# Two constants of a kernel's planner: a later count for GpSimd's copies, and a shorter lead for scores

## The chip, the core and the metric

The kernel runs on one core of one Trainium2 chip. The metric is the device time of one execution in microseconds (us); lower is better. A core has five engines that each work through their own list of instructions in order and meet at semaphores: TensorE (PE in the profile; its weight loads are shown apart as PEld), VectorE (DVE), ScalarE (ACT), GpSimd (POOL) and SyncE (SP, which here only issues DMAs).

## The reference

Attention with talking heads, and a feed-forward layer behind it:

```python
scores = scale * np.matmul(q, k.transpose(0, 1, 3, 2))        # 8 batches, 12 heads, 448 x 448, head_dim 64
scores = np.einsum('bhij,hg->bgij', scores, w_pre)            # heads are mixed before the softmax
attn = softmax(scores, axis=-1)
attn = np.einsum('bhij,hg->bgij', attn, w_post)               # and after it
x = np.matmul(attn, v)                                        # -> 3584 tokens x 768
h = np.maximum(x @ w_in, 0.0)                                 # 768 -> 2048
out = h * h @ w_out                                           # 2048 -> 768
```

## The kernel before

**The work.** Each of the 8 batches is cut into 45 chunks of ten query rows for all twelve heads (120 rows of the array; a few chunks are smaller). A chunk goes through a fixed sequence:

- scores by matmul (L732) into PSUM, copied to SBUF as `snat` by VectorE or ScalarE (L533, L535); there are two `snat` buffers, and a new block of scores may be copied in only when the relayouts that read the old one have landed;
- a relayout by DMA from `snat` into one of 14 buffers `sch` (L763, issued by SP), so that the twelve heads of ten queries lie in one tile;
- the mix of heads by matmul (L892, or in pairs on quarter arrays L838), the row minimum on VectorE (`mn`, L903), the exponential on ScalarE (`es`, L906), the reciprocal of the sums on VectorE (`rc`, L913, once for two chunks);
- scaling of the mixing weights by that reciprocal on GpSimd (`wq`, L916, one instruction for a chunk);
- the matmul of `wq` and `es` (L923, four for a chunk; the text calls it the second mix), its eviction (`atb`), and with all chunks of a half the product with the values (L969).

The feed-forward layer (L1028 for w_in, L1067 for w_out, squares on GpSimd L1049) works on 128 to 256 tokens at a time; it is TensorE's filler between the chunks. The mode in which TensorE's array is split changes with the operation: L838 and most of L732 run on quarter arrays (four matmuls side by side), L969 on two halves, all others on the whole array.

**Keys and queries.** From batch 2 on (`x_piece`), keys and queries of a batch come in two pieces of six heads. GpSimd copies each piece into pair order, three copies for keys (`kn`) and three for queries (`qn`), L659. Then SP issues a transposing DMA of the piece (L672 into `kt`, L678 into `qz`). There is one `kn` and one `qn`, so that the copies of a piece must wait until the transpose of the piece before has landed; each `kt` and `qz` has two buffers, one for each piece, so that a transpose must wait until the scores of the batch before have read them.

**Order.** The kernel has no loop whose order is the program's order. All operations are added to a planner with a list of what they depend on, a cost in ns for each engine and a priority. `Planner.run` plays them against a clock of its own: an engine takes the ready operation of the lowest priority number, is busy for its cost, and what depends on it becomes ready after a further latency. The order in which the planner started the operations is the order that each engine gets. Its costs and latencies are thus used only to choose that order; on the chip each instruction waits for its real semaphores. Three points matter:

- `AHEAD` (7.7) is the number of chunks by which scores (L737) and relayouts (L777, L797) run ahead of the mix that they serve, in the priority.
- A copy of keys or queries depends on the load (`k_in`, `q_in`) and on the transpose of the piece before (`tk_op`, `tq_op`). `ck` and `cq` are the lists of these copies. `NEAR_LAST` (2e6) is their priority; scaling has about its chunk's number, the feed-forward squares 1e6, so of all that is ready on GpSimd the copies come last.
- While TensorE would idle in the first 130 us of the planner's clock, and its share of work is low, the planner puts in matmuls on zeroes (`still`, L1292), which only keep the array at work.

Of the kernel before, what the change touches and what calls it, by code (L numbers as in the profile page):

```python
# [39 lines left out]
NEAR, TURN_SP = {"POOL": 640}, 1500  # L40
PIECE = NPAIR // 2
NE = 6
NSCH = 14
AHEAD = 7.7
FIFO = 50
IDLE_NS, IDLE_COLS, IDLE_FROM, IDLE_END, IDLE_LOW = 112, 256, 1300, 130000, 0.62
SPELL, PHASE, DROP, RISE = 3413, 1700, 0.4, 0.8
# [5 lines left out]
LATER = 2  # L53
ONSET, ONSET_IDLE, ONSET_FROM = 2500, 2500, 20000
NEAR_LAST = 2e6
OSTEP = 2
GS, ONE = [(0, 1, 2)], [(0,), (1,), (2,)]
STAY = {ROWS: 2, COLS: 6, BOTH: 8}
# [69 lines left out]
class Planner:  # L128
# [8 lines left out]
    def add(self, eng, ns, pri, fn, deps=(), lat=60, bank=None, frees=None, mode=0):  # L137
        op = Op(eng if isinstance(eng, dict) else {eng: ns}, lat, pri, fn, list(deps), bank, frees, mode)
        self.ops.append(op)
        return op  # L140
# [199 lines left out]
def kernel(  # L340
# [199 lines left out]
    add = pl.add  # L540
# [13 lines left out]
    q_in, k_in, v_in = {}, {}, {}  # L554
    def keep(key, fn):
        def go(*got):
            for key_, slot in zip(key if isinstance(key, list) else [key], got):
                slots[key_] = slot
            fn(*got)
        return go  # L560
# [17 lines left out]
    def used(b, piece):  # L578
        i = 2 * b + piece - NSLOT
        far = prep_op + [m_op[n] for n in direct] + [score_ops[0, 0, p] for p in range(NPAIR)] if b == 1 else []  # L580
        return far + [score_ops[i // 2, NJ, PIECE * (i % 2) + x] for x in range(PIECE)] if i >= 0 else []
# [74 lines left out]
    tq_op, tk_op = {}, {}  # L656

    def near(eng, out_, in_):
        (nc.gpsimd if eng == "POOL" else nc.vector).tensor_copy(out=out_, in_=in_)  # L659

    def x_piece(b, g):
        i = (2 * b + g) % NSLOT
        h0 = 2 * PIECE * g

        def pair_k(eng, a):
            near(eng, kn[:, :, 2 * a:2 * a + 2, :], ks[:, h0 + 2 * a:h0 + 2 * a + 2, :, :].rearrange("p h j d -> p j h d"))

        def pair_q(eng, a):
            near(eng, qn[:, :, 2 * a:2 * a + 2, :], qs[:, h0 + 2 * a:h0 + 2 * a + 2, :, :].rearrange("p h r d -> p r h d"))

        def turn_k():
            nc.sync.dma_start(  # L672
                out=kt[i][:, :, :, :].rearrange("p j a c -> p (j a) c"),
                in_=kn[:, :, :, :].rearrange("p j h d -> p (j h d)"), transpose=True,
            )

        def turn_q():
            nc.sync.dma_start(  # L678
                out=qz[i][:, :, :, :].rearrange("p r a c -> p (r a) c"),
                in_=qn[:, :, :, :].rearrange("p r h d -> p (r h d)"), transpose=True,  # L680
            )

        pri = b * NCHUNK - 24 + 4.5 * g
        old = used(b, g)
        ck = [
            add(NEAR, 0, NEAR_LAST, lambda eng="POOL", a=a: pair_k(eng, a), [k_in[b, g], tk_op.get(2 * b + g - 1)], lat=80)
            for a in range(PIECE)
        ]
        cq = [
            add(NEAR, 0, NEAR_LAST, lambda eng="POOL", a=a: pair_q(eng, a), [q_in[b, g], tq_op.get(2 * b + g - 1)], lat=80)  # L690
            for a in range(PIECE)
        ]
        sk = add("SP", 2300 if b == 2 else (2700 if g == 0 else TURN_SP + 100), pri, turn_k, ck + old)
        sq = add("SP", 2000 if b == 2 else (2400 if g == 0 else TURN_SP), pri, turn_q, cq + old)
        k_ = tk_op[2 * b + g] = pl.moved("DMA", 60, 26, 26, 0, [sk], 400)
        q_ = tq_op[2 * b + g] = pl.moved("DMA", 60, 23, 23, 0, [sq], 400)
        for first_, last_ in ((ck[0], k_), (cq[0], q_)):
            first_.turns, last_.turns = 1, -1
        for p in range(PIECE * g, PIECE * g + PIECE):
            ready[b, p] = [[k_]] + [[k_, q_]] * NJ  # L700
            got_op[b, p] = ck + cq

    def place_of(b, c):
        return b * NCHUNK + (ORDER0.index(c) if b == 0 else c)
# [6 lines left out]
    def is_direct(b, c):  # L711
        return b == 0 and C0[1] <= c <= C0[2]
# [5 lines left out]
    def score(b, r, group):  # L718
# [17 lines left out]
        first = min(place_of(b, c) for c in range(C0[r], (C0 + [NCHUNK])[r + 1]) if not is_direct(b, c)) - b * NCHUNK  # L736
        pri = b * NCHUNK + first - AHEAD - 0.6 - (0.7 if r == 0 else 1.4) * (NPAIR - p)  # L737
        n = b * (NJ + 1) + r - 2
# [30 lines left out]
    def relayout(b, c):  # L769
# [6 lines left out]
        deps = list(scopy[b, r]) + (list(scopy[b, r - 1]) if r == 1 and cc == 0 else [])  # L776
        pri = n - AHEAD  # L777
        if r == 2 and cc == 0:
# [15 lines left out]
        else:  # L794
            o = cc - 1
            if b >= PAIR_FROM:
                pri = n - o % (2 * PAIRS) + 0.1 * (o % (2 * PAIRS)) - AHEAD  # L797
            o, step = (2 * CI * (o // 2) + o % 2, 2) if b >= PAIR_FROM else (o, CPR)
# [212 lines left out]
    def unit(pair, ui):  # L1011
# [11 lines left out]
        for f0 in range(0, FT, nf):  # L1023
            key = ("f", ix, "h", f0)
            for j in range(nf):
                def mms(slot, f0=f0, j=j):
                    for c2 in range(NPAIR):
                        nc.tensor.matmul(  # L1028
                            slot[:, j * w:(j + 1) * w], lhsT=w1[c2][:, (f0 + j) * 128:(f0 + j + 1) * 128],
                            rhs=xt[:, c2, a:z], start=(c2 == 0), stop=(c2 == NPAIR - 1),  # L1030
                        )
# [27 lines left out]
        for mt in range(w // 128):  # L1059
            whole = not (z == W2B and mt == 1 and pair == B // 2 - 1)  # L1060
            cuts = [0, 384, DMODEL] if whole else [0, 384, 640, DMODEL]
            for nt, (c0, c1) in enumerate(zip(cuts, cuts[1:])):
                key = ("f", ix, "o", mt, nt)
                for f0 in range(0, FT, OSTEP):
                    def mms(slot, f0=f0, mt=mt, c0=c0, c1=c1):
                        for ft in range(f0, f0 + OSTEP):
                            nc.tensor.matmul(  # L1067
# [4 lines left out]
                    if f0 == 0:  # L1072
                        prev = add("PE", (12 + (c1 - c0) * 5 // 3) * OSTEP / 4, fill + 20 + 4 * mt + 2 * nt, keep(key, mms),
                                   [prev] + sq_op[ix][0:max(1, OSTEP // nf)] + w2_in[0:1 if ix < SOON else 4], lat=0, bank=key)
                    else:
                        prev = add("PE", (12 + (c1 - c0) * 5 // 3) * OSTEP / 4, FILL, lambda key=key, mms=mms: mms(slots[key]), [prev, w2_in[f0 // 4]] + sq_op[ix][0:(f0 + OSTEP + nf - 1) // nf], lat=0)
                    o_op[ix].append(prev)
# [163 lines left out]
    def next_batch(b):  # L1241
        n0 = b * NCHUNK
        if b < 2:
            for p in range(NPAIR):
                t_qk(b, p)
            t_tail(b, 0)
            t_tail(b, 1)
        else:
            for g in range(2):
                x_piece(b, g)  # L1250
            x_tail(b)
# [81 lines left out]
```

## Time and profile before

| | before |
|---|---|
| median of 3 runs | 574.48 us (573.99 to 575.98) |
| the profiled execution's own time | 574.91 us |
| its span, first to last instruction | 572.9 us |
| mean granted clock of TensorE | 0.997 |
| DVE busy | 496.8 us (87%) |
| ACT busy | 450.1 us (79%) |
| POOL busy | 365.2 us (64%) |
| relayouts `sch<-snat` of the common shape | 318 DMAs of 105 KB |
| transposes | 12 into `kt`, 12 into `qz`, 6 into `zt` |

Lines of the timeline read: start in us, length in us, engine, line, operation, tiles, shapes, and behind `x` how many like it were merged; in brackets the idle time of the engine just before, and what ended it. Lines of the waits read: who waited, for whom, us in total, how many times, the longest. Lines of windows give for each stretch of the span the busy time of each engine with the number of instructions, then the clock granted to TensorE (1.00 is full speed), the share of the DMA engines and the bytes moved per second. The ends of matmuls are modelled, so that TensorE's busy time hides short gaps; the distance from the start of one matmul to the start of the next does not.

### The profile page before, as it was taken

How to read it: one execution, taken by the hardware profiler on the slowest of the kernel's cores; microseconds unless marked ns; L12 is line 12 of the kernel's file. 1: busy time of each engine (PE TensorE's matmuls, PEld its weight loads, DVE VectorE, ACT ScalarE, POOL GpSimd, SP SyncE). 2: the span in 40 equal slices, each digit the busy share in tenths (PEclk: the TensorE clock that was granted, in tenths of full speed). 3: DMA queues.
4: the chain of work that ended last, by engine and by line, in shares of the span. 5: the costliest groups of instructions: out<-in, count | busy, mean ns of one | idle time of the engine just before them, and what ended most of it. 6: DMA issues, size and time to landing. Idle time of an engine off the chain costs nothing.

```text
span 572.9 us, 17961 instructions
## 1 busy us (share of the span) xinstructions
PE 560.0 (98%) x6335; PEld 398.4 (70%) x6335; DVE 496.8 (87%) x1110; ACT 450.1 (79%) x1185; POOL 365.2 (64%) x677
## 2 busy tenths in 40 slices
PE   7999889999999999999999999999999999999997
PEld 4767676777677586767668676767758676767785
DVE  7999889988989999998898888989899999989442
ACT  5799879988888889887887888977988889888100
POOL 8767247768577458855777556955688544746451
PEclk9999989999999999999999999999999999999999
DMA  9999849965798559873897639975398646432011
GB/s 137 212 188 223 162 97 169 186 142 130 128 209 169 125 140 181 161 167 103 144 189 132 177 92 147 188 138 164 90 195 147 163 132 123 127 84 71 1 56 55
DMA packets 129949, 80.85 MB, mean 141 GB/s; under 512 B 59274, under 2 KB 126588, under 8 KB 129860
## 3 DMA queue, kind: packets, MB, share of 16 engines
q1 hardware_dynamic: 80756, 46.29, 36.4%
q0 software_dynamic: 49104, 33.43, 36.1%
q8 instruction: 49, 0.80, 0.6%
q14 instruction: 40, 0.33, 0.2%
HBM read 45.61 MB, written 11.01 MB: 99 GB/s over the span
## 4 chain that ended last, share of the span: by engine, by line
PE 86%; DVE 5%; DMA 3%; ACT 2%; issue 1%; POOL 1%; DVEq 0%; POOLq 0%; ACTq 0%
PE bank L1067 26%; PE bank L1028 25%; PE bank L923 14%; PE bank L969 6%; PE bank L732 6%; PE bank L838 5%; PE bank L892 3%; DMA sch<-snat 2%; DVE mn L903 2%; DMA qs<-in_q_dram 1%; ACT es L906 1%; PE bank L898 1%; DVE osb L881 1%; DVE atb L533 1%; DVE hr L1042 1%
## 5 line engine op out<-in xcount | busy, mean ns | idle before, releaser
L906 ACT ACTIVATE es<-bank,mn 124x448 bf16<-124x448 f32 (+1 forms) x360 | 228.9, 644 | 28.5 <-DVE mn L903 24.6
L903 DVE TENSOR_REDUCE mn<-bank 124x1 f32<-124x448 f32 (+1 forms) x360 | 209.2, 614 | 4.7 <-PE bank L838 3.8
L1067 PE MATMUL bank<-w,h 128*128 128x384 bf16 (+2 forms) x912 | 178.0, 323 | 0.3 <-ACT osb L535 0.2
L1028 PE MATMUL bank<-xt,w 128*128 128x256 bf16 (+1 forms) x1632 | 165.7, 255 | 0.7 <-DVE hr L1042 0.3
L1028 PEld LDWEIGHTS <-w 128*128 128x128 bf16 x1632 | 134.3, 98 | 25.8 <-issue 12.4
L1049 POOL TENSOR_TENSOR h<-hr 128x512 bf16<-128x512 f32 x112 | 116.2, 1040 | 43.8 <-DVE hr L1042 23.1
L916 POOL TENSOR_SCALAR wq<-wback_two,rc 124x120 bf16<-124x120 f32 x252 | 89.5, 366 | 65.9 <-DVE rc L913 52.0
L923 PEld LDWEIGHTS <-es 124*112 124x112 bf16 (+2 forms) x1440 | 107.4, 130 | 33.7 <-issue 8.1
L923 PE MATMUL bank<-wq,es 124*112 124x120 bf16 (+2 forms) x1440 | 119.6, 218 | 4.4 <-POOL wq L916 2.0
L533 DVE CAST atb<-bank 112x480 bf16<-112x480 f32 (+3 forms) x193 | 113.7, 603 | 10.7 <-PE bank L923 9.9
L1067 PEld LDWEIGHTS <-h 128*128 128x128 bf16 x912 | 80.2, 98 | 55.7 <-issue 16.8
L535 ACT CAST atb<-bank 112x480 bf16<-112x480 f32 (+2 forms) x190 | 103.1, 552 | 19.3 <-PE bank L923 17.8
L533 DVE CAST snat<-bank 128x448 bf16<-128x448 f32 x155 | 92.2, 615 | 4.1 <-DMA sch<-snat 2.8
L535 ACT CAST snat<-bank 128x448 bf16<-128x448 f32 x163 | 82.5, 547 | 11.4 <-PE bank L732 8.2
L906 ACT ACTIVATION_READ_ACCUMULATOR es<-bank,mn 124x1 f32 (+1 forms) x360 | 75.3, 209 | 0.0
L1042 DVE TENSOR_SCALAR hr<-bank 128x512 f32<-128x512 f32 x75 | 51.7, 690 | 22.9 <-PE bank L1028 16.7
L916 POOL TENSOR_SCALAR wq<-wback,rc 124x120 bf16<-124x120 f32 (+1 forms) x94 | 33.8, 367 | 43.9 <-DVE rc L913 30.4
L732 PE MATMUL bank<-kt,qz 64*64 64x448 bf16 (+1 forms) x528 | 46.6, 362 | 0.2
L838 PE MATMUL bank<-sch,wmix 64*64 64x448 bf16 x504 | 41.7, 360 | 0.0
L1091 POOL DMA_DIRECT2D out_dram<-osb x33 | 19.6, 595 | 34.4 <-DVE osb L533 17.2
L969 PE MATMUL bank<-atb,vs 112*64 112x192 bf16 (+3 forms) x864 | 40.7, 250 | 0.0
L969 PEld LDWEIGHTS <-vs 112*64 112x64 bf16 x864 | 36.6, 110 | 4.8 <-issue 4.4
(80 smaller groups left out, 400.2 us busy)
## 6 DMA issues: line engine op xcount, KB each, us to landing
sch<-snat SPq DMA_DIRECT2D x318, 105.0 KB
out_dram<-osb POOLq DMA_DIRECT2D x21, 384.0 KB, 3.5
vs<-in_v_dram POOLq DMA_DIRECT2D x16, 336.0 KB, 7.2
ks<-in_k_dram POOLq DMA_DIRECT2D x14, 336.0 KB, 8.4
qs<-in_q_dram POOLq DMA_DIRECT2D x14, 288.0 KB, 6.2
w<-in_moe_w_in_dram POOLq DMA_DIRECT2D x6, 512.0 KB, 13.2
w<-in_moe_w_out_dram POOLq DMA_DIRECT2D x4, 768.0 KB, 20.3
out_dram<-osb POOLq DMA_DIRECT2D x8, 192.0 KB, 4.9
```

Of the source, the lines that this page charges most:

```text
L533: nc.vector.tensor_copy(out=out_, in_=in_)
L535: nc.scalar.copy(out=out_, in_=in_)
L732: nc.tensor.matmul(slot[m0:m1, 0:S], lhsT=lhsT[:, m0:m1], rhs=kt[i][half, :, at_, :], start=True, stop=True,)
L838: nc.tensor.matmul(got[i + x][o0:o1, 0:S], lhsT=w[k0:k1, c0:c0 + o1 - o0], rhs=srcs[i + y][k0:k1, :], start=True, stop=True,)
L903: nc.vector.tensor_reduce(out=mn[i][0:rows, :], in_=slots[mk][0:rows, 0:S], axis=AX.X, op=ALU.min)
L906: nc.scalar.activation(out=es[i][0:rows, 0:S], in_=slots[mk][0:rows, 0:S], func=ACT.Exp, scale=-1.0, bias=mn[i][0:rows, 0:1], accum_out=sm ...
L916: nc.gpsimd.tensor_scalar(out=wq[i][0:rows, :, 0:ns], in0=back[0:rows, :, 0:ns], scalar1=rc[i // 2][0:rows, i % 2:i % 2 + 1], scalar2=1.0, ...
L923: nc.tensor.matmul(slot[0:P_KEYS, jb * H * ns:(jb + 1) * H * ns], lhsT=es[i][0:rows, jb * P_KEYS:(jb + 1) * P_KEYS], rhs=wq[i][0:rows, :, ...
L969: nc.tensor.matmul(v_[64 * hh:64 * hh + 64, i, 0:x1 - x0], lhsT=vs[:, 2 * c2 + hh, jb, :], rhs=atb[half][:, jb, 2 * c2 + hh, x0:x1], start ...
L1028: nc.tensor.matmul(slot[:, j * w:(j + 1) * w], lhsT=w1[c2][:, (f0 + j) * 128:(f0 + j + 1) * 128], rhs=xt[:, c2, a:z], start=(c2 == 0), sto ...
L1049: nc.gpsimd.tensor_tensor(out=h2_[:, f0:f0 + nf, 0:w], in0=hr[gi % 2][:, :].rearrange("p (f c) -> p f c", f=nf), in1=hr[gi % 2][:, :].rear ...
L1067: nc.tensor.matmul(slot[:, 0:c1 - c0], lhsT=h2_[:, ft, mt * 128:(mt + 1) * 128], rhs=w2[:, ft, c0:c1], start=(ft == 0), stop=(ft == FT - 1),)
```

## The change

Two edits. `AHEAD` goes from 7.7 to 7.0. And from batch 2 on, the planner is told that what a copy of keys or queries depends on (load, and transpose of the piece before) ends 3000 ns later than it is counted otherwise: an operation of no cost on an engine of its own, with a latency of 3000, stands between. It issues no instruction. The dependencies of every instruction on the chip are those of before; only their order in each engine's list differs.

```diff
-AHEAD = 7.7
+AHEAD = 7.0
...
+NEAR_LATE, NEAR_LATE_FROM = 3000, 2
...
+        def late(what, op):
+            if b < NEAR_LATE_FROM or op is None:
+                return op
+            return add("LATE%s%d" % (what, 2 * b + g), 0, 0, lambda: None, [op], lat=NEAR_LATE)
+
+        k_late = [late("k", k_in[b, g]), late("tk", tk_op.get(2 * b + g - 1))]
+        q_late = [late("q", q_in[b, g]), late("tq", tq_op.get(2 * b + g - 1))]
         ck = [
-            add(NEAR, 0, NEAR_LAST, lambda eng="POOL", a=a: pair_k(eng, a), [k_in[b, g], tk_op.get(2 * b + g - 1)], lat=80)
+            add(NEAR, 0, NEAR_LAST, lambda eng="POOL", a=a: pair_k(eng, a), k_late, lat=80)
             for a in range(PIECE)
         ]
         cq = [
-            add(NEAR, 0, NEAR_LAST, lambda eng="POOL", a=a: pair_q(eng, a), [q_in[b, g], tq_op.get(2 * b + g - 1)], lat=80)
+            add(NEAR, 0, NEAR_LAST, lambda eng="POOL", a=a: pair_q(eng, a), q_late, lat=80)
             for a in range(PIECE)
         ]
```

## The prediction

> **What bounds the kernel now.** I read the page's busy times first, then TensorE's waits, the timeline where they stand, and the windows.
>
> ```profile
> PE 560.0 (98%) x6335; PEld 398.4 (70%) x6335; DVE 496.8 (87%) x1110; ACT 450.1 (79%) x1185; POOL 365.2 (64%) x677
> ```
>
> TensorE is busy all but 12.9 us of 572.9. Since its ends are modelled, I also went by starts: a matmul of 384 columns takes 0.163 us in a run of its own kind (8 in 1.30 us in the chain of waits), one of 128 columns 0.056 (24 in 1.34). Where the start of the next stands beyond that, the array stood still. Taken over all 6335 matmuls, such gaps hold 69 us: 19 in steps under 60 ns, 34 in 340 gaps of 60 to 150 ns, 16 in 41 longer ones (some 5 of these before 15 us, 7 between 35 and 85, under 5 in the 485 us after). The middle group is changes of the array's mode:
>
> ```profile
> 417.00 0.36 PE L838 MATMUL bank<-sch,wmix 64*64 64x448 bf16 x4
> 417.29 0.50 PE L1067 MATMUL bank<-w,h 128*128 128x384 bf16 x2
> ```
>
> Four quarter-array matmuls of 448 columns run side by side and are through 0.19 us after 417.00; the next kind starts at 417.29, 0.10 late with nothing to wait for. Behind 90 us there are 272 such changes with a median of 0.096 us. So the kernel is bound by TensorE's stream of work; at stake are the number of mode changes and the few real waits. From 90 to 540 us the waits for GpSimd's scaling are these:
>
> ```profile
> PE bank L923 <- POOL wq L916: 0.7, 2, 0.4
> ```
>
> That is all that the planner's new count can take away on TensorE in the stretch where it acts. The largest wait is elsewhere, at 70 us, before any of the copies:
>
> ```profile
> 66.96 0.57 PE L732 MATMUL bank<-kt,qz 64*64 64x448 bf16 x8
> 67.46 0.42 PE L923 MATMUL bank<-wq,es 124*112 124x120 bf16 x4
> 67.85 1.50 PE L1028 MATMUL bank<-xt,w 128*128 128x128 bf16 x24
> 70.72 0.42 PE L923 MATMUL bank<-wq,es 124*112 124x120 bf16 x4 [1.37 <-DVE snat L533]
> ...
> 72.91 2.77 PE L1028 MATMUL bank<-xt,w 128*128 128x128 bf16 x24
> ```
> ```profile
> 70.03 0.62 DVE L533 CAST snat<-bank 128x448 bf16<-128x448 f32 x1 [2.57 <-DMA sch<-snat]
> ```
>
> The scores at 66.96 are to be copied into a `snat` buffer that the last relayout of batch 0 (issued at 58.5, landed near 69.9 while the w_out loads ran) still reads. VectorE sits 2.57 us in front of that copy, ScalarE 2.13, and the chunks behind it wait too, TensorE 1.37 us. And the same 24 matmuls that took 1.50 us at 67.85 take 2.77 at 72.91:
>
> ```profile
> 70.00:73.00 3.00, 2.14 (x18) 1.24 (x19) 2.96 (x8) 3.00 (x8) 1.00 (x3) 0.88 0.76 151
> 73.00:76.00 3.00, 3.00 (x34) 2.94 (x35) 1.61 (x5) 0.81 (x3) 1.40 (x3) 0.55 0.55 152
> ```
>
> The clock falls to half at 72.27 and is back at 75.68, a stretch of 3.41 us; it is the only one but the very end. In the 3.41 us ahead of it the array streamed 36% of the time; in the two first stretches of the kernel, at 49 and 50%, it was not taken down.
>
> **The change part by part.** What moves is read from the order of the instructions in the two built programs. Copies stay 72, transposes 30, relayouts as many as before; TensorE gets 50 filler matmuls for 45.
>
> *Copies behind scaling.* 60 of the 72 copies stand behind more scalings than before, 4 behind fewer. The case it is meant for is here once:
>
> ```profile
> 381.52 0.96 POOL L659 COPY qn<-qs 128x384 bf16<-128x384 bf16 x2 [3.21 <-DMA qz<-qn]
> 382.46 0.71 POOL L916 TENSOR_SCALAR wq<-wback_two,rc 124x120 bf16<-124x120 f32 x2
> ```
> ```profile
> 382.88 0.37 PE L923 MATMUL bank<-wq,es 124*112 124x120 bf16 x4 [0.38 <-POOL wq L916]
> ```
>
> GpSimd waits 3.21 us in front of two copies, the scaling behind them starts at 382.46, TensorE waits 0.38. Copies wait for a transpose twice in the whole run (4.4 us on GpSimd). The other 0.3 us (at 451) stands behind no copy. So this part is worth 0.4 us: **-0.4**, between 0 and -0.7.
>
> *Transposes and what waits for them.* Later copies push the transposes behind up to 9 more relayouts on SP, and the relayouts no longer queue behind a transpose that waits (SP waits 28 us for copies now). A relayout's landing lies 4 to 10 us (median of a 20 us stretch) ahead of the mix that reads it, at least 1.2; 0.7 chunks at 1.6 us (572.9 / 360) take 1.1 of it. No cost. The scores that read a transpose are moved too. For the second piece of keys, where landing to first score is 0.1 to 2.8 us now, the scalings between the last key copy and that score go from 24 to 30 over the six batches: more room. For the first piece they go from 62 to 38: less. Counted in TensorE's work between the last score that reads the old keys and the first that reads the new ones, batch 2 falls from 16.4 to 12.7 us and batch 3 from 16.2 to 11.4; the slack now is 6.3 and 7.8 us, which leaves 2.6 and 3.0. I take **0**, with a bound of +4.5 (a rival below) and none below zero, for no TensorE wait on these keys is there to lose.
>
> *Mode changes.* In the order they go from 308 to 324: the pairs of quarter-array work come in smaller groups. 16 x 0.096 = **+1.5**. None of the engines hides these; between +0.5 (a third of them in places where TensorE waits anyway) and +1.6.
>
> *Fillers.* Five more of 256 columns are 0.5 us of array time; they stand in one row of 16 where now 9 stand in front of a wait of 1.02 us. **0**, between 0 and +0.5.
>
> *The wait at 70 us.* Counted from the same place (36 scores, 34 second mixes and 40 mixes done; 65.5 us now), the next scores stand behind 1.4 us of TensorE's work now and behind 5.0 after: three groups of feed-forward matmuls go ahead of them. They would start 3.6 us later, the copies with them; VectorE's wait is 2.57, so it is gone with 1 us to spare. With it goes TensorE's 1.37 us, and, since the array streams on, the stretch at half clock: 2.77 - 1.50 = 1.3. Together **-2.7**, from 0 (the landing comes later too) to -3.2 (with the 0.3 and 0.2 us by which the scores at 71.06 and the mix at 72.47 come late). It is not given back at once: VectorE, busy 3.00 of 3.00 us from 79 to 85, bounds that stretch, but it has the 2.57 us and another 1.39 at 76 idle now, and moves ahead with the chunks.
>
> Clock, a rule against this: the Trainium skill, "TensorE: Matmul & The Clock Gate", Part 1, has the clock go down after an idle window of about 3.4 us, and advises against gaps over some 3 us. No gap here is over 1.6 us, and yet the clock fell; the 36% row says that a share is enough. By the rule the half clock would have another cause and stay, and the sum below would lose 1.3.
>
> The sum against the profiled execution: 574.9 - 0.4 + 1.5 - 2.7 = 573.3. The median is 0.43 below that execution; 574.48 - 1.6 = **572.9**.
>
> **The rivals.**
>
> *The knot at 70 us stays* because the last relayout lands later as well (it shares the DMA engines with loads that end at 75.7). Then -0.4 + 1.5 and up to 0.5 of fillers: 575.6 to 576.1. For it: the row of 16 fillers, by which the planner sees no shorter idle time there. Against it: SP's order is the same for the first 63 relayouts.
>
> *The first piece of keys comes late* in batches 2 and 3 (scores L732 near 120 and 185 us). The last key copy stands behind the 62nd and the 108th scaling instead of the 58th and 104th, and from there to the scores lie 11.0 and 5.7 us of TensorE's work (16.3 and 14.7 now). Copy, issue and landing took 12.2 us (101.6 to 113.8) and, from the issue alone, 7.9 (168.8 to 176.7). GpSimd ran 0.8 us ahead of TensorE at the first place and 4.7 at the second; if it is only 0.8 at both, TensorE stalls 0.4 and 2.6 us, and with one more stretch at half clock 1.5: 4.5 in all, **577.4**. It decides if the first key transpose of batch 3 lands more than 3 us later than TensorE reaches its scores. Against it: the planner moves those scores by its own count, which is now the slower one for copies.
>
> *TensorE isn't the bound*, VectorE is, and mode changes cost nothing: -0.4 - 2.7, **571.4**. Against it: from 538 to 573 us TensorE works alone in three unbroken runs, and the gaps of 0.096 show up start to start. The Trainium skill, "Perfetto Trace Analysis", section "Identifying the Most-Contended Engine", says that matmul busy time is a poor measure and takes weight loads instead; by those, 70%, VectorE's 87% would be the bound. The starts of this trace disagree with it.
>
> *The clock stays down* at 72 us though the wait goes: 572.9 + 1.3 = **574.2**.
>
> *The change doesn't do what it says*: its aim is worth 0.4 us in any case; without it each figure is that much higher. It is within the ranges.
>
> **How the numbers follow.** The knot undone, 0.52, with a range of 570.9 to 574.3; knot stays 0.20; keys late 0.15; TensorE not the bound 0.08; clock stays down 0.05. A measurement of this kernel can tell about 0.3% (1.7 us) from no change: under 572.8 is faster, over 576.2 slower. The likeliest case splits 0.32 to 0.20 into faster and same, because the clock and 0.5 us of late starts can add to it; the knot's stay 0.11 same, 0.09 slower; keys late is slower, TensorE not the bound faster, the clock same. Faster 0.40, same 0.36, slower 0.24. The range takes in all but the outer ends: 570.9 to 577.6.
>
> **What would show it.** In the profile of the changed kernel: no bracket of VectorE or ScalarE for DMA `sch<-snat` over 1 us between 65 and 75 us; granted clock 1.00 in all windows of 60 to 90 us; L1028's groups of 24 there at 1.3 to 1.5 us each; 324 mode changes at 0.096; GpSimd's copies without the 3.21 us bracket; no TensorE wait for scaling over 0.3 us behind 90 us. It is wrong if L732 in batches 2 and 3 waits for DMA `kt<-kn`, if a second stretch at half clock shows, or if the gaps behind 90 us, under 5 us now, grow by more than 1.5.

## The result, and the profile after

The changed kernel takes **571.6 us** (570.89 to 571.90, 5 runs) where the kernel before takes 574.48: a ratio of **0.9943, 95% interval 0.9925 to 0.9961**. The forecast was 572.9, in a range of 570.9 to 577.6. The profiled execution of the changed kernel took 571.90 us (574.91 before), its span is 570.1. The diff shifts line numbers: L732 is now L741, L838 is L847, L892 is L901, L916 is L925, L923 is L932, L1028 is L1037, L533 is L534, L659 is L660, L1292 is L1301. Edits of the experiments shift lines too; each view has the numbers of its own kernel.

Busy times, first part of the page of the changed kernel:

```profile
PE 561.1 (98%) x6340; PEld 398.5 (70%) x6340; DVE 500.8 (88%) x1109; ACT 446.4 (78%) x1186; POOL 363.0 (64%) x677
```

TensorE's busy time went up by 1.1 us while the span fell by 2.8, so fewer waits must have more than paid for more work.

The place at 70 us, TensorE's timeline and below it one line of VectorE's, and then the windows, all of the changed kernel:

```profile
68.66 1.50 PE L1037 MATMUL bank<-xt,w 128*128 128x128 bf16 x24
70.00 0.35 PE L901 MATMUL bank<-sch,wmix 124*128 124x448 bf16 x1
70.20 1.50 PE L1037 MATMUL bank<-xt,w 128*128 128x128 bf16 x24
71.63 0.76 PE L741 MATMUL bank<-kt,qz 64*64 64x448 bf16 x12
...
77.38 1.91 PE L1301 MATMUL bank<-still 128*128 128x256 bf16 x16
80.41 0.37 PE L932 MATMUL bank<-wq,es 124*112 124x120 bf16 x4 [1.12 <-POOL wq L925]
```
```profile
72.42 1.68 DVE L534 CAST snat<-bank 128x448 bf16<-128x448 f32 x3
```
```profile
70.00:73.00 3.00, 3.00 (x52) 2.37 (x50) 2.49 (x6) 2.75 (x9) 2.73 (x7) 1.00 0.79 143
73.00:76.00 3.00, 3.00 (x47) 2.12 (x45) 2.98 (x8) 2.61 (x7) 2.35 (x4) 1.00 0.69 178
```

The scores that stood at 66.96 now stand at 71.63, behind the feed-forward groups; the copy into `snat` has no bracket any more; the clock stays at 1.00, and a group of 24 takes 1.50 us. But part is given back a few us later: TensorE does 16 fillers and then still waits 1.12 us for scaling at 80.41.

GpSimd at the place of the 3.21 us bracket, and TensorE's waits from 90 to 540 us (who waited for whom: us in total, times, longest), both of the changed kernel:

```profile
378.49 1.71 POOL L660 COPY kn<-ks 112x512 bf16<-112x512 bf16 x3
380.15 0.95 POOL L660 COPY qn<-qs 128x384 bf16<-128x384 bf16 x2
382.33 0.70 POOL L925 TENSOR_SCALAR wq<-wback_two,rc 124x120 bf16<-124x120 f32 x2 [1.23 <-PE bank L847]
```
```profile
PE bank L1037 <- DVE hr L1051: 0.3, 2, 0.2
```

The copies no longer wait for a transpose, and behind 90 us no wait for scaling is left in the list.

**An account of the lost time.** To see where the gain comes from I priced the whole of TensorE's stream: 2.4 columns per ns, about what the 0.163 us for 384 columns give, four quarter-array matmuls as one, and 0.096 us for each mode change. The start of a given second mix less the price of all that stands ahead of it is what TensorE has lost up to there (mixes are counted from 0, so that 45 stand ahead of the 45th). The work up to the 34th, 45th or last mix can differ between two orders; the lost time takes that out.

| | priced stream | lost up to 34 mixes (68 us) | up to 45 (83 us) | up to the last | of that, behind 45 |
|---|---|---|---|---|---|
| before | 543.0 | 9.1 | 14.8 | 26.5 | 11.7 |
| changed | 545.1 | 10.4 | 12.4 | 21.7 | 9.3 |

More stream, +2.1; less lost up to the 45th mix, -2.4; less lost behind it, -2.4. Together -2.7, and the executions differ by 3.0. The levels depend on the price: the table's is 13.6 us above columns and mode changes alone, by which the streams are 529.4 and 531.5, the loss up to the 45th mix 16.4 and 14.1, behind it 22.9 and 20.5. The differences hardly depend on it. How far one execution can be trusted is seen up to the 45th mix, where the order of before ran in five profiles: it lost 13.7 to 14.9.

### The profile page after: what moved, and what is told of

It is laid out like the page before. It is cut to its first block, busy times and chain, and to the rows that moved or that the text cites. A ratio compares the mean times of both kernels' runs of the same rounds, so it can differ in the third digit from the quotient of the medians.

```text
span 570.1 us, 17924 instructions
## 1 busy us (share of the span) xinstructions
PE 561.1 (98%) x6340; PEld 398.5 (70%) x6340; DVE 500.8 (88%) x1109; ACT 446.4 (78%) x1186; POOL 363.0 (64%) x677
## 4 chain that ended last, share of the span: by engine, by line
PE 90%; DVE 6%; POOL 1%; DMA 1%; issue 1%; ACT 0%; DVEq 0%; POOLq 0%; ACTq 0%
PE bank L1076 27%; PE bank L1037 25%; PE bank L932 13%; PE bank L741 7%; PE bank L978 7%; PE bank L847 5%; PE bank L901 3%; PE bank L907 2%; DVE mn L912 1%; DVE snat L534 1%; DMA sch<-snat 1%; DVE atb L534 1%; PE bank L1301 1%; DVE hr L1051 1%; DVE osb L890 1%
## 5 line engine op out<-in xcount | busy, mean ns | idle before, releaser
L1037 PE MATMUL bank<-xt,w 128*128 128x256 bf16 (+1 forms) x1632 | 164.1, 254 | 0.6 <-DVE hr L1051 0.3
L1037 PEld LDWEIGHTS <-w 128*128 128x128 bf16 x1632 | 132.8, 98 | 25.8 <-issue 12.2
L925 POOL TENSOR_SCALAR wq<-wback_two,rc 124x120 bf16<-124x120 f32 x252 | 88.8, 362 | 86.3 <-DVE rc L922 60.2
L932 PEld LDWEIGHTS <-es 124*112 124x112 bf16 (+2 forms) x1440 | 108.0, 129 | 32.5 <-issue 8.8
L534 DVE CAST atb<-bank 112x480 bf16<-112x480 f32 (+3 forms) x196 | 119.1, 617 | 10.6 <-PE bank L932 9.6
L932 PE MATMUL bank<-wq,es 124*112 124x120 bf16 (+2 forms) x1440 | 120.2, 217 | 2.0 <-POOL wq L925 1.5
L536 ACT CAST atb<-bank 112x480 bf16<-112x480 f32 (+3 forms) x187 | 98.2, 539 | 16.1 <-PE bank L932 14.5
L536 ACT CAST snat<-bank 128x448 bf16<-128x448 f32 x168 | 84.6, 543 | 11.4 <-PE bank L741 10.6
L534 DVE CAST snat<-bank 128x448 bf16<-128x448 f32 x150 | 89.8, 614 | 0.8 <-PE bank L741 0.3
L1051 DVE TENSOR_SCALAR hr<-bank 128x512 f32<-128x512 f32 x82 | 56.6, 690 | 21.1 <-PE bank L1037 15.7
L925 POOL TENSOR_SCALAR wq<-wback,rc 124x120 bf16<-124x120 f32 (+1 forms) x94 | 33.6, 365 | 39.3 <-DVE rc L922 26.1
L741 PE MATMUL bank<-kt,qz 64*64 64x448 bf16 (+1 forms) x528 | 44.6, 361 | 0.1
L847 PE MATMUL bank<-sch,wmix 64*64 64x448 bf16 x504 | 42.7, 363 | 0.0
L1100 POOL DMA_DIRECT2D out_dram<-osb x33 | 19.9, 604 | 29.9 <-DVE osb L534 16.4
```

What stands on the lines that cost most here:

```text
L534: nc.vector.tensor_copy(out=out_, in_=in_)
L536: nc.scalar.copy(out=out_, in_=in_)
L741: nc.tensor.matmul(slot[m0:m1, 0:S], lhsT=lhsT[:, m0:m1], rhs=kt[i][half, :, at_, :], start=True, stop=True,)
L847: nc.tensor.matmul(got[i + x][o0:o1, 0:S], lhsT=w[k0:k1, c0:c0 + o1 - o0], rhs=srcs[i + y][k0:k1, :], start=True, stop=True,)
L925: nc.gpsimd.tensor_scalar(out=wq[i][0:rows, :, 0:ns], in0=back[0:rows, :, 0:ns], scalar1=rc[i // 2][0:rows, i % 2:i % 2 + 1], scalar2=1.0, ...
L932: nc.tensor.matmul(slot[0:P_KEYS, jb * H * ns:(jb + 1) * H * ns], lhsT=es[i][0:rows, jb * P_KEYS:(jb + 1) * P_KEYS], rhs=wq[i][0:rows, :, ...
```

## The experiments

**Theory:** the shorter lead moves the scores behind other work and so dissolves the knot at 70 us; the late count for copies takes waits away behind it. **Rivals:** the knot's gain is given back in the stretch up to 85 us, which VectorE and ScalarE bound; TensorE is not the bound; or the gain behind 85 us is not the count's doing but only the order in which the planner happened to fall. In all twelve kernels the whole output is computed.

**1 and 2. Each edit alone.** `AHEAD = 7.0` in the kernel before; the late count with `AHEAD = 7.7`.

> The kernel before with the shorter lead alone (7.0 for 7.7); the count for copies is left as it was. Theory 1 (the gain comes from the scores of batch 1 that no longer block VectorE and ScalarE at 70 us, and from the clock that stays up there): the lead alone bears it. 574.5 less 2.7 for wait and clock, plus 0.6 for 6 more mode changes (314 in its order): 572.4, no half clock between 60 and 90 us. Theory 2 (the gain comes from the later count: real waits of TensorE behind 90 us went from 4.9 to 1.9 us): it gains nothing, 574.5 or more, and its waits behind 90 us stay near 5 us.

> The kernel before with the later count alone; the lead stays 7.7. Its order is that of the kernel before up to batch 2, so that the wait at 70 us stands. Theory 1: 574.5 less 0.4 to 0.7 for the waits for scaling, plus 0.4 for 4 more mode changes: 574.1 to 574.5, with the half clock at 72 us as before. Theory 2: about 572, with the waits behind 90 us down to some 2 us.

Measured: the lead alone 572.38 us, ratio 0.9967 (0.9950 to 0.9985); the count alone 573.39, ratio 0.9983 (0.9967 to 1.0000). Together -0.33% and -0.17% make -0.50%, the change has -0.57%: within the intervals the edits add. Time lost up to the 45th mix: 12.1 with the lead, 13.7 with the count, 14.8 before. Behind it: 11.8 with the lead, 9.8 with the count, 11.7 before. So the lead earns in the first 85 us and the count behind them; the 13.7 of the count is no gain of its own, for its order on TensorE is that of before up to 109 us. (For experiments 1 to 4 the ratios of the record lie 0.1 to 0.2% above those of the medians against 575.09, the kernel before in that session; the text goes by the former.) With the count alone VectorE still waits its 2.6 us at 70 us; no half clock followed in that execution (see the last section).

**3. The knot undone by hand, lead and count as before.** The four score groups behind the knot and their eight copies are emitted later:

```diff
+        late_s, late_c = [score_ops[1, 1, p] for p in range(4)], scopy[1, 1][0:8]
+        moved = late_s[0:2] + late_c[0:4] + late_s[2:4] + late_c[4:8]
...
+            if op is at_op[37]:
+                for m in moved:
+                    held[id(m)][0].fn(*held[id(m)][1])
```

> The kernel before with its own order, in which only four groups of scores of batch 1 and the eight copies of them are put behind two groups of feed-forward matmuls, ahead of the second mix of chunk 37. Nothing else moves. Theory 1: wait (1.4 us) and half clock (1.3) go, two mode changes go too (0.2): 571.6. Rival (what is won at 70 us is given back where VectorE bounds the stretch from 79 to 85 us): 574.0 or more, with a longer wait of the second mix at 80 us.

Measured: 574.11 us, ratio 0.9999 (0.9984 to 1.0014); by the medians 0.9983: little or nothing. Its VectorE and TensorE, timelines, and TensorE's wait as it was before:

```profile
72.82 2.75 DVE L533 CAST snat<-bank 128x448 bf16<-128x448 f32 x5 [1.63 <-PE bank L732]
```
```profile
73.39 1.01 PE L732 MATMUL bank<-kt,qz 64*64 64x448 bf16 x8 [0.47 <-ACT snat L535]
...
80.54 0.37 PE L923 MATMUL bank<-wq,es 124*112 124x120 bf16 x4 [1.02 <-POOL wq L916]
```
```profile
81.31 0.37 PE L923 MATMUL bank<-wq,es 124*112 124x120 bf16 x4 [1.02 <-POOL wq L916]
```

The wait for `sch<-snat` is gone, but VectorE now waits 1.63 us for the later scores, the copies come in one lump of five, TensorE waits for them, and the wait of 1.02 at 80.54 is where it was (81.31 before). The lost time up to the 45th mix is 14.2, within the 13.7 to 14.9 of the order of before. The rival "given back" is right for this local repair: scores that are moved for one knot only move the wait. What the lead does is more: it re-plans all that stands around, and loses 12.1.

**4. Twelve fillers ahead of the mix that waits at 70 us**, order as before:

```diff
+            if n == 35:
+                for _ in range(12):
+                    stand(slot, 0)
```

> The kernel before with its own order and 12 matmuls of 256 columns on zeroes ahead of the second mix of chunk 35, into the bank that it then overwrites: 1.3 us of work where TensorE stands still for 1.4. The wait of VectorE and ScalarE stays. If the clock goes by the share of time in which the array works (36% there), it stays up: 574.5 less 1.3, 573.2, with no half clock at 72 us. If it needs a whole idle window, the half clock has another cause and stays: 574.5. If the second mix's bank comes free only with the scores' copies, the fillers wait like it: 574.5 to 575.8 and half clock.

Measured: 575.21 us, ratio 1.0024 (1.0010 to 1.0038). The fillers did not fill the gap, for they write a bank that VectorE had yet to read (TensorE's timeline):

```profile
71.11 1.47 PE L1295 MATMUL bank<-still 128*128 128x256 bf16 x12 [1.35 <-DVE snat L533]
```

They wait 1.35 us as the mix did without them. Their 1.3 us of array time were hidden at first: the 45th mix starts at 83.6, as it does in experiment 7, whose order is that of before up to there. So in this stretch TensorE is not the bound. Where the 0.24% of the whole program arise I did not find; by the medians of the session they are 0.02%. On the clock its profile tells nothing, for this order went without half clock in other executions too (last section). Over all executions of the session there is a hint: 2 of 12 here, and 2 of 12 in experiment 3, have a mean granted clock of 0.997 or less, against 17 of 35 of the kernel before.

**5 and 6. The price of a mode change.** In 48 second mixes, between 162 and 518 us, one more matmul of 120 columns stands ahead of the fourth: on a quarter array (two more mode changes each), or on the whole array (none). It writes where the fourth then writes.

```diff
+                if jb == 3 and ns == CI and 100 <= n < 340 and n % 5 == 0:
+                    nc.tensor.matmul(slot[0:64, 360:480], lhsT=still[0:64, 0:64], rhs=still[0:64, 0:120], ...)
```

> The kernel before with one more matmul of 120 columns on zeroes in 48 of the second mixes of batches 2 to 7, on a quarter of the array, into columns that the next matmul overwrites. Each comes between matmuls on the whole array and thus makes two mode changes more. If a change costs 0.096 us wherever it stands and TensorE is the bound: 48 x (0.05 + 0.19) = 11.5 us, 586.0. If TensorE has room (VectorE being the bound), it is nearer to the same kernel with matmuls on the whole array.

> As the kernel with 48 quarter matmuls, but the added matmuls run on the whole array, without a mode change: 48 x 0.055 = 2.6 us, 577.1, if TensorE is the bound; 574.5 if it has room. The difference of the two is the price of 96 mode changes: 9.2 us by 0.096 each.

Measured: quarter 587.56 us, ratio 1.0220 (1.0197 to 1.0244); whole 577.50, ratio 1.0040 (1.0023 to 1.0056). The difference is 10.06 us for 96 changes, 0.105 each. And 48 matmuls of 120 columns, 0.05 us each by their columns, make the whole program 2.5 us longer, 0.052 each, though VectorE is busy 87%. So between 162 and 518 us TensorE is the bound: that rival falls, and 16 mode changes more are 1.5 to 1.7 us.

**7. Copies alone, moved behind scaling.** Order as before, but 61 of the 72 copies are emitted behind the next two scalings that stand ahead of their transpose:

```diff
...
+                behind = [i_ for i_ in scalings if at[id(op)] < i_ < at[id(turn_)]][:2]
+                place = max(behind[-1] if behind else at[id(op)], last)
...
```

> The kernel before with its own order, in which only GpSimd's copies are put behind the next two scalings, where these come before the copy's transpose; 61 of 72 move. All other lists stay. Theory A (scaling ahead of copies is what the later count gains by): the wait for scaling at 383 us and those like it go, and the time is that of the later count alone, about 0.2% under the kernel before. Theory B (the later count gains because the planner lays out TensorE, VectorE and ScalarE anew, not by the copies' places): no change, 0.0 to -0.4 us, and the waits for scaling elsewhere stay as they are; a copy that is now 0.7 us later can make the second piece's keys late, where they have 0.1 to 2.8 us.

Measured: 578.67 us, ratio 1.0060 (1.0040 to 1.0081): slower, which neither theory had named. TensorE's waits from 104 to 540 us, its timeline and GpSimd's at the largest one:

```profile
PE bank L925 <- POOL wq L918: 3.1, 4, 2.2
```
```profile
318.48 0.37 PE L925 MATMUL bank<-wq,es 124*112 124x120 bf16 x4 [2.15 <-POOL wq L918]
```
```profile
313.67 1.72 POOL L660 COPY kn<-ks 112x512 bf16<-112x512 bf16 x3
315.37 0.36 POOL L918 TENSOR_SCALAR wq<-wback_two,rc 124x120 bf16<-124x120 f32 x1
315.68 1.40 POOL L660 COPY qn<-qs 128x384 bf16<-128x384 bf16 x3
317.05 1.04 POOL L1051 TENSOR_TENSOR h<-hr 128x512 bf16<-128x512 f32 x1
318.06 0.71 POOL L918 TENSOR_SCALAR wq<-wback_two,rc 124x120 bf16<-124x120 f32 x2
```

The copies are put off past one scaling, and then stand in a lump ahead of the next: 1.40 us of copies and 1.04 of squares come before the scaling at 318.06 for which TensorE waits 2.15. Here the half clock follows, from 320.0 for 3.4 us. The words of the change, copies behind scaling, are therefore no gain by themselves. These are not the places that the planner gives the copies, though: it moves them by another rule, and scaling, squares and scores with them. That the late count of experiment 2 earned by these other places is likely, but not shown: no run has the planner's places for copies alone.

**8 to 12. Neighbours.** If the gain were the edits' doing, leads close to 7.0 should give about the same. Only `AHEAD` differs in these.

> The changed kernel with a lead of 7.1 instead of 7.0, a neighbour that re-plans all orders: 309 mode changes for 324. Theory 1 (later scores and later copies gain by what they move): 571.6 less 1.4 for the mode changes, 570.2 to 571.6. Theory 3 (any new order scatters by one or two us, and 7.0 fell well): anywhere from 571 to 575, with other waits behind 90 us than the 1.9 us of the changed kernel.

> The changed kernel with AHEAD 6.9 in place of 7.0 and the same late count; the whole computation is done. It has 310 mode changes (324 in the changed kernel). The 7.1 run stood at 573.88 with real waits of 3.6 us behind 105 us, the changed kernel at 571.6 with 1.3. Theory that the changed kernel's place among its neighbours is partly chance of where the planner's order fell: the stretch up to 85 us is as short as in the changed kernel (the loss at the 46th second mix within 0.5 of 12.4 us), waits behind 105 us lie anywhere from 1.3 to 3.8, and the time follows them: 571.6 - 14 x 0.096 = 570.3 with 1.3 us of waits, 572.8 with 3.8. Rival, the lead of 7.0 us and the late count fit each other: every other lead gives 573.5 or more.

> The changed kernel with AHEAD 6.3, as far from 7.0 as that is from the 7.7 of before; the whole computation is done; 320 mode changes. Theory that a shorter lead is worth something by itself, because scores then come when VectorE and ScalarE have room: the loss at the 46th second mix falls again, from 12.4 to 11.5 or less, and the time is 570.5 to 572. Rival, the lead is used up: scores and their exponentials come late, TensorE waits for es or for the scaling of wq more often than 1 us in sum behind 105 us, and the time is 573 to 576.

> The kernel before (early count for copies) with AHEAD 6.9; the whole computation is done; 322 mode changes, 54 fillers. With the late count the same lead was slower than before (577.5). Theory that the late count is what fails at 6.9: here the time stays near the 572.4 of lead 7.0 with the early count, 571.5 to 573.5, and the stretch up to 85 us is short again. Rival, leads beside each other scatter by some 3 us whatever the count, since each gives another order and another few waits: the time may lie anywhere from 571 to 577, and the difference comes from waits for single landings behind 105 us, while the first 85 us keep their gain.

> The kernel before with AHEAD 7.1; the whole computation is done; 305 mode changes, 50 fillers. Theory that a lead near 7 us is worth 2 us whatever is around it: 571.5 to 573. Rival (scatter): anywhere from 571 to 577; by its mode changes alone, 9 fewer than at 7.0, it would be 0.9 us faster than the 572.4 there, so that whatever it has above 571.5 is waits.

Measured, ratio to the kernel before with its interval, and the lost time up to the 45th mix and behind it:

| lead | early count (as before) | lost | late count | lost |
|---|---|---|---|---|
| 7.7 | 1 | 14.8 + 11.7 | 0.9983 (0.9967 to 1.0000) | 13.7 + 9.8 |
| 7.1 | 0.9966 (0.9950 to 0.9983) | 12.1 + 11.6 | 0.9986 (0.9973 to 0.9998) | 12.1 + 12.9 |
| 7.0 | 0.9967 (0.9950 to 0.9985) | 12.1 + 11.8 | **0.9943 (0.9925 to 0.9961)** | 12.4 + 9.3 |
| 6.9 | 1.0191 (1.0171 to 1.0211) | 12.4 + 23.6 | 1.0049 (1.0024 to 1.0075) | 12.9 + 16.8 |
| 6.3 | not run | | 1.0038 (1.0023 to 1.0053) | 12.6 + 13.9 |

The first part of the theory holds in all seven kernels with a lead of 7.1 or less: 12.1 to 12.9 us are lost up to the 45th mix, against 13.7 to 14.8 at 7.7 in the table. They are three orders rather than seven: on TensorE, the four kernels at 7.0 and 7.1 share one up to 98 us, and the two at 6.9 another up to 97 us. The second part does not hold everywhere: the late count takes 1.9, 2.5 and 6.8 us of loss away at 7.7, 7.0 and 6.9, but adds 1.3 at 7.1. And a step of a tenth of a chunk, from 7.0 to 6.9, costs 1% with the late count and 2% with the early one: more than the whole change brings. Four expectations fell outright: that 7.1 with the late count would give 570.2 to 571.6 (573.88), that 6.9 with it would lie between 570.3 and 572.8 by its waits (577.54), that 6.9 with the early count would stay near 572 (586.49, beyond the 571 to 577 of its rival too), and that a lead of 6.3 would be worth more than 7.0 (576.85). No version here beats the changed kernel.

One place where 6.9 loses is seen on SP around 105 us, where the first piece of batch 2 is transposed. The late count at 6.9, SP and then TensorE:

```profile
106.40 2.89 SPq L643 DMA_TRANSPOSE zt<-qt  x1
109.40 4.58 SPq L673 DMA_TRANSPOSE kt<-kn  x1
114.07 2.28 SPq L679 DMA_TRANSPOSE qz<-qn  x1
116.40 13.95 SPq L772 DMA_DIRECT2D sch<-snat  x14
```
```profile
122.66 0.35 PE L901 MATMUL bank<-sch,wmix 124*128 124x448 bf16 x1 [1.99 <-DMA sch<-snat]
```

SP spends 10 us on three transposes; the relayout behind them is issued at 116.40, lands at 122.5, and TensorE waits 1.99 us for it. In the changed kernel the same three take 7.3 us and no relayout comes late:

```profile
104.93 4.29 SPq L673 DMA_TRANSPOSE kt<-kn  x1
109.34 1.38 SPq L643 DMA_TRANSPOSE zt<-qt  x1
110.81 1.38 SPq L679 DMA_TRANSPOSE qz<-qn  x1
112.24 11.83 SPq L772 DMA_DIRECT2D sch<-snat  x12
```

With the early count at 6.9 there are five relayouts between 100 and 140 us that land less than 0.15 us ahead of the mix that reads them (none in the changed kernel, one in each of the early counts at 7.0 and 7.1). The worst of them, on TensorE, and the window behind it:

```profile
133.48 0.37 PE L923 MATMUL bank<-wq,es 124*112 124x120 bf16 x4 [1.23 <-POOL wq L916]
134.04 0.38 PE L838 MATMUL bank<-sch,wmix 64*64 64x448 bf16 x2 [0.20 <-DMA sch<-snat]
136.31 0.56 PE L838 MATMUL bank<-sch,wmix 64*60 64x448 bf16 x2 [1.89 <-DMA sch<-snat]
```
```profile
136.00:140.00 4.00, 3.69 (x22) 2.32 (x25) 1.73 (x4) 0.72 (x2) 0.61 (x2) 0.57 0.62 165
```

Three waits in 4 us, then half clock (0.57 in that window): between the 60th and the 90th mix this kernel loses 10 us, where the changed one loses 0.9.

## Why the prediction was right, and where it was not

- **What bounds the kernel: right where it was tried, from 162 to 518 us.** Whole-array matmuls added to the stream cost their own time (experiment 6), and the price of a mode change read from starts, 0.096 us, came out at 0.105 when it was measured by itself. From 70 to 85 us TensorE does not bound it (experiment 4); that VectorE and ScalarE do is read from their waits and busy times, and experiment 3 fits it.
- **Mode changes, +1.5: right.** The changed kernel has 324; at 0.096 to 0.105 the 16 are 1.5 to 1.7 us.
- **Fillers, 0 to +0.5: the upper end.** They stand in one row of 16, and TensorE waits 1.12 us behind them, but the priced stream grew by them too; where the wait would be without them no run shows.
- **The wait at 70 us, -2.7: right in mechanism, right in size by the two profiles.** Every sign that was named came: no bracket over 1 us for `sch<-snat`, clock 1.00, groups at 1.50 us. The stretch up to the 45th mix lost 2.4 us less. But "it is not given back at once" was half wrong: experiment 3 shows that the same knot undone without re-planning gives all or nearly all of it back, and in the changed kernel the wait for scaling at 80.41 grew from 1.02 to 1.12, fillers ahead of it from 9 to 16. And the 1.3 us for the half clock were counted as sure, where they belong to about half of the executions (last section); against the same order at full clock (13.7, 14.2 and 14.6 lost up to the 45th mix in experiments 2, 7 and 6) the lead's 12.1 is a gain of 1.6 to 2.5.
- **Copies behind scaling, -0.4: the step that was mis-sized.** "That is all that the planner's new count can take away on TensorE in the stretch where it acts" looked at waits for scaling that a listing names. Waits beyond a mode change's price fell by 2.1 us behind 105 us (3.35 to 1.26), the lost time behind the 45th mix by 2.4. Six waits of second mixes, 1.43 us together beyond the price of a mode change, were among them; the listing has two of them, and the others, 0.17 to 0.31 from start to start, show only in the starts. Four of the six, 1.2 us, are for scaling; at 136.69 and 146.34 the weights of the mix, `es`, came last from ScalarE. And the mechanism was hardly that copies stand behind scaling (experiment 7 does that by its own rule and is slower); the other places that the planner chose with them are what is left, not shown by a run of their own.
- **Keys that come late, 0.15:** not in the changed kernel; the first piece of keys lands 3.1 to 5.8 us ahead of its scores (3.2 to 8.1 before). In batches 2 and 3 it is 4.3 and 4.9, above the 2.6 and 3.0 that were worked out. At a lead of 6.3 TensorE does wait 1.0 us for `kt<-kn` at 130.9 (the second piece), and at 6.9 with the early count 1.3 us in two places.
- **The sum.** +1.5, -2.7 and -0.4 gave 573.3 for the profiled execution. Measured terms are +2.1 for the stream, -2.4 and -2.4. The errors were 0.6, 0.3 and 2.0, the last one the cause of a forecast that was 1.3 us too high. The first two went the other way and took 0.9 of it back, which was luck.
- **What the prediction did not see at all** is how thin the ground is. It weighed the new order as a property of the edits. The neighbours show that a tenth of a chunk in the lead, from 7.0 to 6.9, moves the time by 1 to 2%, in part through relayouts that land just in time or just late, to which it gave no cost. That this order came out well was read rightly from its own lists; that edits of this kind bring something was not shown by that.

What stays open: why the late count costs 1.3 us at 7.1, and why it takes 6.8 of 23.6 us of loss away at 6.9; I did not follow single waits there back to single copies.

## What to carry to other kernels

Where a planner fixes the order, a changed constant is a new draw: read the order it gives, place by place, and run the neighbours before believing in the constant. A local repair of a wait (moving what comes too early) gave next to nothing here, where the engines around it were full; the waits must also be gone a few us later. On a busy TensorE, count mode changes and short waits from start to start, down to a tenth of a us: the six waits of second mixes were worth 1.4 us here, twice what the listing showed of them.

## What the runs showed of the hardware

In these profiles the half clock goes with the phase of a gap as well as with its length. In five of fourteen profiles TensorE fell to half clock in mid-run, for 3.41 us each time, and each time at a whole number of 3.413 us stretches behind the first moment of full clock:

| kernel | full clock from | half clock from | stretches between | array's share in the stretch ahead |
|---|---|---|---|---|
| before | 4.00 | 72.27 | 20.00 | 0.30 |
| 5 (quarter) | 4.42 | 72.69 | 20.00 | 0.27 |
| 7 (copies) | 9.40 | 320.01 | 91.00 | 0.38 |
| 11 (early, 6.9) | 10.07 | 136.36 | 37.00 | 0.11 |
| 9 (late, 6.9) | 4.80 | 11.62 | 2.00 | 0.53 |

The share counts columns streamed, a quarter-array matmul as a quarter (a stricter count than the prediction's 36%). Stretches on the same grid that kept full clock go down to 0.30, 0.36 and 0.38, so the share alone, as these records allow it to be counted, does not separate the two. The same order with the same knot kept full clock at 72 us where its grid lay elsewhere (experiments 2, 6 and 7, full clock from 9.4 to 10.4). Those executions pay at the start instead: up to the 34th mix they lose 9.6 to 9.8 us, the two with the earlier grid 8.7 and 9.1.

How often it comes is told by the mean granted clock of every execution, where one stretch of 3.41 us makes 0.997. Of 94 executions of the kernel before, in the four sessions of the experiments, 49 have 0.997 or less, with a median of 575.25 us; the other 45 have 573.93. So the 1.3 us of the prediction are about right for one execution, and wrong as a sure loss. Of the five kernels with leads of 7.1, 7.0 and 6.3, which show no wait for `sch<-snat` over 1 us at 70 us, 7 of 53 executions have 0.997 or less; of the two at 6.9, 11 of 13. An estimate from these shares, (49/94 - 7/53) x 1.3, is 0.5 us of the change's 2.9.

The Trainium skill, "TensorE: Matmul & The Clock Gate", Part 1, describes a free-running window of 3413 ns. Every row above agrees with that length. The Trainium skill's table of the two states there has the clock go down after an idle window of about 3.4 us. These falls do not agree: no gap in TensorE's starts ahead of them is over 2.4 us, and the array streamed in every one of the windows.
